# Routing attention and a gated feed-forward block on one core: score masks put ahead of their products, and two query tiles cut at 448 keys

## The chip, the cores and the metric

The kernel runs on one core of one Trainium2 chip. The metric is device time in microseconds (us) from the first to the last moment of one execution; the median of several runs is given. The engines are TensorE (PE; its weight loads are shown apart as PEld), VectorE (DVE), ScalarE (ACT), GpSimd (POOL) and SyncE (SP), which issues DMAs.

## The reference

Two blocks follow one another. The first is attention in which a query sees only the keys of its own cluster; the second is a feed-forward block with an activation of its own.

```
# B, H, S, D = 4, 8, 768, 64; 16 clusters for each head
q_assign = argmax(normalised q . normalised centroids)
k_assign = argmax(normalised k . normalised centroids)
mask   = q_assign[..., :, None] == k_assign[..., None, :]
scores = where(mask, q @ k.T / sqrt(D), -1e9)
scores = scores - max(scores, axis=-1)
attn   = exp(scores) / (sum(exp(scores)) + 1e-9)
x      = attn @ v, turned to (3072 tokens, 512)

h  = x @ w_in                       # 512 x 2048
sp = max(h, 0) + log1p(exp(-|h|))
out = (h * erf(sp)) @ w_out         # 2048 x 512
```

## The kernel before

The attention works on 16 pairs of heads (`p`), the two heads of a pair in the two halves of the 128 partitions (64 rows each). A pair has 6 tiles of 128 queries and 6 tiles of 128 keys. The program order of every engine is the order of the code (`InOrder`); nothing is reordered by a planner.

**Units.** A unit (`units`, line 542) is one half of the queries (384) against one tile of 128 keys; a pair has 12. Its scores lie in a tile `sc` of two PSUM banks, one for each head, and there are two such tiles (`ps_s`, line 177). `products(u)` multiplies keys by queries in float32 over 64 rows a head and opens the banks; `scores(u)` adds the cluster masks in bf16 and closes them; `curve(u)` takes the exponential on ACT and writes `pr`; `accumulate(u)` adds it up on POOL; `attend(u)` multiplies it with the values, one period later, into `turned`.

**The masks.** `km` holds the one-hot clusters of the keys and `qm` those of the queries, scaled so that their product is far below zero where clusters differ. They occupy 32 of the 64 rows of a head, and each of them is there twice: rows 0 to 31, where the first row of `qm` also holds the shift (the row maximum of the scores), and rows 32 to 63, without it. So `scores(u)` with 32 rows uses rows 0 to 31 of each half, and the maxima can use rows 32 to 63.

**The maxima.** Each query needs the maximum over its keys before its exponentials. `maxima_step` computes a piece: `passes("qv", "kv", ...)` multiplies a bf16 copy of 128 queries by some of the keys into the PSUM tile `wide` (two banks, one for each head; there is one such tile), `passes("qm", "km", ...)` adds the cluster masks, and DVE reduces the piece to a column of `nmx`. With `behind=True` it is a generator that stops between these parts, and its masks use rows 32 to 63; otherwise it runs through and they use all 64 rows. A query tile `t` is done in two pieces, the first over `KEYS[t]` keys and the second over the rest of the 768. After the second piece of tile 2 and tile 5, `into_rows` turns the maxima and four DMAs on SP's queue put them into `qm` as the shift of that half.

**A period.** `period(p, i)` (line 1393), six for each pair, runs two units, `u` and `u+1`, and two maxima steps. Its order on PE is

1. first step, run through (`step_ahead(p, 2*i)`): the second piece of a query tile, 64-row masks;
2. `products(u)`, `products(u+1)`;
3. second step (`step_ahead(p, 2*i+1, True)`): the first piece of the next query tile; its similarities, then `scores(u)`, then its masks, then `scores(u+1)`;
4. at some `i` a mask of the next pair (`masks`; at i=2 a narrow one in place 2, on 32 rows);
5. `attend` for the two units of the period before.

The steps of a period run ahead of the units that need them. For pairs from 1 on the pieces are, by period:

| i | first step: tile, keys before | second step: tile, keys before |
|---|---|---|
| 0 | 3, 256 | 4, 512 |
| 1 | 4, 256 | 5, 512 |
| 2 | 5, 256 | 0 of the next pair, 384 |
| 3 | 0, 384 | 1, 512 |
| 4 | 1, 256 | 2, 512 |
| 5 | 2, 256 | 3, 512 |

The feed-forward block after the attention is PE work in 128 by 128 tiles; the change does not touch it.

Of the kernel before, what the change touches and what calls it, by code (L numbers as in the profile page):

```python
# [9 lines left out]
F32 = mybir.dt.float32  # L10
# [9 lines left out]
P = 128  # L20
B, H, S, D = 4, 8, 768, 64
C = 16
NJ = S // P
Q = 32
NB = S // Q
HW = S // 2
QW = HW // 2
TW = QW + 1
HJ = NJ // 2
HP = H // 2  # L30
KEYS = (384, 512, 512, 512, 512, 512)
FIRST_KEYS = (256, 256, 352, 384, 256, 352)
JOINED = (
    ((0, 0, 0, 512),), ((0, 1, 512, 768), (1, 0, 0, 256)), ((1, 1, 256, 768),), ((2, 0, 0, 512),), ((2, 1, 512, 768),),
# [101 lines left out]
def kernel(  # L136
# [37 lines left out]
    def passing(name, bufs, **kw):  # L174
        return attention.enter_context(tc.tile_pool(name=name, bufs=bufs, **kw))

    ps_s = passing("ps_s", 2, space=PSUM)
# [30 lines left out]
    rows = [{nm: const.tile([P, S], F32, name=f"{nm}T{i}") for nm in "qk"} for i in range(2)]  # L208
# [109 lines left out]
    def sign(n):  # L318
        hi, _, upper = steps[n]
        ae.activation(out=upper, in_=hi, func=ACT.Prelu, scale=2.0**-25, alpha=2.0**90)  # L320
# [12 lines left out]
    for e in range(2):  # L333
        for n in range(2):
            r = e * D + n * Q
# [89 lines left out]
    def vectors(p, nm):  # L425
        if p < NPAIR:
            ae.copy(out=pairs[p][nm + "v"], in_=pairs[p][nm + "T"])

    def masks(p, nm, half, bank, narrow=False, copied_by=ae):

        if p >= NPAIR:
            return lambda: None
        st = pairs[p]
        cols = slice(half * HW, (half + 1) * HW)
        r, hot = slice(0, D) if nm == "q" else slice(D, P), st["hotT"]
        picked = pick[r, half]
        if narrow:
            r = slice(r.start + Q, r.stop)
            picked = pick[r, 1]
            hot = hot if half else st["aside"]  # L440
        won = bank[:, 0:HW]
        te.matmul(won, lhsT=picked, rhs=hot[r], start=True, stop=True)
        if nm == "q":
            return lambda: ae.activation(out=st["qm"][:, cols], in_=won, func=ACT.Relu)
        if copied_by is ve:
            return lambda: ve.tensor_scalar(
                out=st["km"][:, cols], in0=won, scalar1=BIG, scalar2=nbig, op0=ALU.mult, op1=ALU.add
            )
        return lambda: ae.activation(
            out=st["km"][:, cols], in_=won, func=ACT.Identity, bias=nbig, scale=BIG  # L450
        )
# [3 lines left out]
    def pieces_of(i, keys_of):  # L455
        t, part = divmod(i, 2)
        return ((t, part, *((0, keys_of[t]), (keys_of[t], S))[part]),)
# [84 lines left out]
    units = [(p, half, j) for p in range(NPAIR) for half in range(2) for j in range(NJ)]  # L542

    sc_of = {}

    def products(u):
        p, half, j = units[u]
        if u in sc_of:
            return
        st = pairs[p]  # L550
        sc = sc_of[u] = ps_s.tile([P, 2, 512], F32, name="sc", tag="s")
        for e in range(2):
            r = slice(e * D, (e + 1) * D)
            te.matmul(
                sc[:, e, 0:HW], lhsT=st["kT"][r, j * P : (j + 1) * P],
                rhs=st["qT"][r, half * HW : (half + 1) * HW], start=True, stop=False,
            )

    def scores(u, rows=Q):

        p, half, j = units[u]
        st = pairs[p]
        sc = sc_of[u]
        assert ("shift", half) in st
        for e in range(2):
            r = slice(e * D, (e + 1) * D)
            r = slice(r.start, r.start + rows)
            te.matmul(
                sc[:, e, 0:HW], lhsT=st["km"][r, j * P : (j + 1) * P],
                rhs=st["qm"][r, half * HW : (half + 1) * HW], start=False, stop=True,  # L570
            )

    def curve(u):
# [795 lines left out]
    def run(work):  # L1369
        for _ in work:  # L1370
            pass
# [3 lines left out]
    def step_ahead(p, i, behind=False):  # L1375
        if p == 0 and i < NJ:
            steps = maxima_step(0, pieces_of(NJ + i, FIRST_KEYS), behind=behind, by_products=True)
        elif p == 0 and i < NJ + len(JOINED):
            steps = maxima_step(1, JOINED[i - NJ], behind=behind)
        else:  # L1380
            p, i = divmod(2 * NJ * p + NJ + 1 + i, 2 * NJ)
            steps = maxima_step(p, pieces_of(i, KEYS), behind=behind) if p < NPAIR else iter(())
        if not behind:
            run(steps)
        return steps
# [7 lines left out]
    def period(p, i):  # L1393
        u = 2 * NJ * p + 2 * i
        n1, n2 = 2 * p - 1, 2 * p
        early = lambda n: 0 <= n < N_EARLY

        def mask(place):
            which = (MASKS if p else FIRST_MASKS).get((i, place))
            if which:  # L1400
                return masks(p + 1, *which, turned[0 if i in (0, 5) else 1], place == 2)
            return lambda: None

        if u > 0:
            for which in turns if i in (0, 3) else ():
                turn(*which)
                turns.remove(which)
            if i == 3 and not p:
                transposes(2, "k")
            if i == 3 and p:  # L1410
                similarities(p + 2)
                routing[0] = choose(p + 2, turned[0], True)
            step_ahead(p, 2 * i)
            if i == 3 and p:
                next(routing[0], None)
            if i == 2:
                transposes(p + 2, "k" if p else "q")
        mask(0)()
        if i == 0 and early(n1 - 1):
            sign(n1 - 1)  # L1420
        elif i == 3 and early(n1):
            sign(n1)
        if i == 4:
            next(routing[0], None)
        next(part[0], None)
        if i == 0 and p:
            run(routing[0])
            transposes(p + 2, "q")
        if u == 2:
            next(routing[0])  # L1430
        products(u)
        mask(3)()
        products(u + 1)
        mask(1)()
        second = step_ahead(p, 2 * i + 1, True) if u > 0 else iter(())
        next(second, None)
        rows = D if u == 0 or u + NJ + 2 >= len(units) else Q
        scores(u, rows)
        next(second, None)
        next(second, None)  # L1440
        next(part[0], None)
        if i == 5 or u == 2:
            next(routing[0], None)
        scores(u + 1, rows)
        later = mask(2)
        if i == 3 and not p:
            similarities(p + 2)
            routing[0] = choose(p + 2, turned[0], True)
        if i == 0:
            later()  # L1450
            curve(u)
        else:
            curve(u)
            later()
        curve(u + 1)
        if u == 0:
            step_ahead(0, 1)
            similarities(1)
            routing[0] = choose(1, turned[1])
            next(routing[0])  # L1460
            vectors(1, "q")
            vectors(1, "k")
        if i == 0 and early(n1 - 1):
            bounded(n1 - 1)
            shifted(n1 - 1)
        elif i == 1 and early(n1):
            size_and_rest(n1)
        elif i == 5 and early(n2):
            rest(n2)
        for _ in range(FORMS.get(p, {}).get(i, 0)):  # L1470
            x_forms.pop(0)() if x_forms else forms.pop(0)[0]()
        if i == 3:
            if not p:
                next(routing[0], None)
            if early(n1):
                bounded(n1)
                shifted(n1)
        elif i == 1:
            load(p + 1, "v", v, vp)
            if p == 0:  # L1480
                run(routing[0])
        elif i == 4:
            vectors(p + 2, "k")
            vectors(p + 2, "q")
        if u > 0:
            if i == 1 and early(n1 - 1):
                summed(n1 - 1)
            elif i == 4 and early(n1):
                summed(n1)
            if i in POOL_FORMS.get(p, ()) and forms:  # L1490
                forms.pop(0)[1]()
            for w in (u - 2, u - 1):
                accumulate(w)
            for w in (u - 2, u - 1):
                attend(w)
            if i == 3:
                next(routing[0], None)
            if i % HJ == 0 and u - 1 != LATE or u - 3 == LATE:
                part[0] = divide(u - 1 - u % NJ)
                next(part[0])  # L1500
        if i == 3 and early(n2):
            size(n2)
# [11 lines left out]
    st = pairs[0]  # L1514
# [56 lines left out]
    u = len(units)  # L1571
# [13 lines left out]
    behind = pool("behind", 1).tile([P, 1], F32, name="behind")  # L1585
# [87 lines left out]
```

## Time and profile before

| | |
|---|---|
| median of 3 runs | 947.51 us (947.37 to 947.69) |
| profiled execution | 948.0 us |
| its span, first to last instruction | 946.3 us |
| PE busy | 939.0 us, 99% |
| DVE busy | 785.0 us, 83% |
| ACT busy | 547.2 us, 58% |
| POOL busy | 505.6 us, 53% |

The time is that of the whole execution; the span is what the hardware profiler saw between the first and the last instruction of one execution. Every instruction that goes through the helper `InOrder` is recorded under its line, L127, so groups are told apart by their tiles: `wide<-kv,qv` are a maxima step's similarities, `wide<-km,qm` its masks, `sc<-qT,kT` the products (for every third pair the operands lie in `more_out`, and the row reads `sc<-more_out`), `sc<-qm,km` the score masks, `turned<-pr,in_v` the value products, `turned<-hotT,pick` a mask of the next pair in the making. A float32 matmul is recorded as two. The shape `64*128` says how many rows and columns of the array a matmul uses.

### The profile page before, as it was taken

Reading aid. Unit: us, or ns where it says so; the run is one execution under the profiler, and the core shown is the slowest. Engines: PE = TensorE matmul, PEld = TensorE weight load, DVE = VectorE, ACT = ScalarE, POOL = GpSimd, SP = SyncE. Lnnn points to the kernel's source line nnn. Section 1 sums busy time; section 2 is a strip of 40 time slices with the busy share of each in tenths; the row PEclk is TensorE's granted clock in tenths of the full one; section 3 lists DMA queues with packets and bytes.
Section 4 is the critical chain, followed back from the end, with each engine's and each line's share of the span. In section 5 each row is a group of like instructions: output and inputs, shape, how many; then the busy total and the mean of one; then the engine's idle time right before and its main releaser. Section 6 shows DMA issues by size and latency. Waiting matters only on the chain.

```text
span 946.3 us, 22340 instructions
## 1 busy us (share of the span) xinstructions
PE 939.0 (99%) x8764; PEld 708.1 (75%) x8764; DVE 785.0 (83%) x1420; ACT 547.2 (58%) x809; POOL 505.6 (53%) x357
## 2 busy tenths in 40 slices
PE   8999999999999999999999999999999999999998
PEld 3555555555555555588888888998999899989987
DVE  7888888888888887869886688689868977897887
ACT  3677777777777777476423543653257236525541
POOL 1688888888888888999118211450063016103600
PEclk9999999999999999999999999999999999999999
DMA  9354455445443621133876248353454336343533
GB/s 217 73 114 112 112 113 111 112 112 111 113 113 69 157 58 36 26 120 124 216 224 238 100 122 214 109 179 112 156 167 135 133 119 206 113 154 123 157 112 111
DMA packets 176352, 123.17 MB, mean 130 GB/s; under 512 B 132600, under 2 KB 143352, under 8 KB 176248
## 3 DMA queue, kind: packets, MB, share of 16 engines
q1 hardware_dynamic: 171880, 116.34, 43.1%
q0 software_dynamic: 1872, 4.98, 3.0%
q8 instruction: 69, 1.13, 0.5%
q10 hardware_dynamic: 2496, 0.43, 0.2%
q14 instruction: 35, 0.29, 0.1%
HBM read 91.78 MB, written 23.33 MB: 122 GB/s over the span
## 4 chain that ended last, share of the span: by engine, by line
PE 98%; DVE 1%; ACT 0%; issue 0%; DVEq 0%
PE bank L127 43%; PE turned L127 32%; PE sc L127 17%; PE wide L127 6%; DVE nmx L127 1%; ACT qm L127 0%; DVE sims L127 0%; ACT km L127 0%; DVE hotT L127 0%; DVE wide L127 0%; DVE hot L127 0%; DVE nbig L127 0%; DVE osb L127 0%; DVEq L1668 0%; DVE lowest L127 0%
## 5 line engine op out<-in xcount | busy, mean ns | idle before, releaser
L127 POOL TENSOR_TENSOR more_out<-more_out,pr 128x768 f32<-128x768 f32 x128 | 217.2, 1697 | 15.8 <-ACT pr L127 6.1
L127 DVE TENSOR_REDUCE nmx<-wide 128x2 f32<-128x512 f32 (+2 forms) x189 | 179.1, 948 | 46.9 <-PE wide L127 45.9
L127 ACT ACTIVATE pr<-sc 128x768 f32<-128x768 f32 x192 | 148.5, 810 | 80.5 <-PE wide L127 73.0
L127 PE MATMUL turned<-pr,in_v 128*32 128x193 f32 x3072 | 145.2, 330 | 0.0
L127 POOL TENSOR_TENSOR g<-g 128x512 f32<-128x512 f32 x36 | 47.2, 1310 | 180.7 <-DVE g L127 178.8
L127 PEld LDWEIGHTS turned<-pr,in_v 128*32 128x32 f32 x3072 | 90.2, 109 | 51.3 <-issue 27.3
L127 DVE TENSOR_TENSOR g<-g 128x512 f32<-128x512 f32 x132 | 90.8, 688 | 22.9 <-PE bank L127 12.2
L127 PE MATMUL sc<-qT,kT 64*128 64x384 f32 x528 | 98.5, 485 | 0.0
L127 DVE TENSOR_TENSOR g<-bank,g 128x256 f32<-128x256 f32 (+1 forms) x128 | 64.7, 531 | 18.1 <-PE bank L127 9.4
L127 PE MATMUL bank<-g_more,g 128*128 128x256 f32 (+1 forms) x328 | 75.8, 374 | 0.0
L127 PE MATMUL bank<-x_own,w_in 128*128 128x128 f32 (+1 forms) x440 | 74.0, 309 | 0.0
L127 ACT ACTIVATE a_s<-g 128x1024 f32<-128x1024 f32 x38 | 39.7, 1056 | 58.0 <-POOL g L127 45.3
L127 POOL TENSOR_TENSOR more_out<-pr,pr 128x768 f32<-128x768 f32 x32 | 59.6, 1864 | 20.1 <-ACT pr L127 20.1
L127 PEld LDWEIGHTS bank<-g_more,g 128*128 128x128 f32 x328 | 61.1, 190 | 8.4 <-DVE g L127 0.4
L127 DVE TENSOR_TENSOR g<-a_s,g 128x512 f32<-128x512 f32 x76 | 65.9, 888 | 0.9 <-ACT a_s L127 0.9
L127 PEld LDWEIGHTS bank<-x_own,w_in 128*128 128x128 f32 x440 | 63.2, 191 | 4.4 <-issue 0.6
L127 PE MATMUL wide<-kv,qv 64*128 64x256 bf16 (+2 forms) x378 | 64.8, 327 | 0.9 <-ACT km L127 0.6
L127 PE MATMUL bank<-w_out,g 128*128 128x256 f32 x280 | 64.5, 379 | 0.0
L127 PEld LDWEIGHTS <-qv 64*128 64x128 bf16 x384 | 23.1, 93 | 52.8 <-issue 37.8
L127 PE MATMUL wide<-km,qm 64*128 64x256 bf16 (+4 forms) x378 | 62.3, 326 | 0.0
L127 ACT ACT_TABLE_LOAD x40 | 51.3, 1283 | 17.6 <-DVE g L127 17.0
L127 PEld LDWEIGHTS sc<-qT,kT 64*128 64x128 f32 x528 | 46.3, 187 | 19.1 <-issue 1.8
(244 smaller groups left out, 1993.0 us busy)
## 6 DMA issues: line engine op xcount, KB each, us to landing
g_more<-b_dram SPq DMA_DIRECT2D x52, 512.0 KB
g_more<-w_dram SPq DMA_DIRECT2D x84, 256.0 KB
x_own<-in_moe_w_in_dram SPq DMA_DIRECT2D x13, 512.0 KB
in_v<-in_v_dram SPq DMA_DIRECT2D x32, 192.0 KB
x_dram<-more_out SPq DMA_DIRECT2D x128, 48.0 KB
x_own<-x_dram SPq DMA_DIRECT2D x6, 1024.0 KB
in_k<-in_k_dram SPq DMA_DIRECT2D x59, 96.0 KB
in_q<-in_q_dram SPq DMA_DIRECT2D x58, 96.0 KB
```

The lines of the kernel that those rows point to most:

```text
L127: ins = getattr(self.engine, name)(*args, **kw)
```

## The change

In four of the six periods (i = 1, 2, 4, 5) of pairs from 1 on, the score masks of the first unit go ahead of its products, between the similarities and the masks of the first maxima step. They open the banks (`start`), and the products, now behind them, close them (`stop`). The first step then runs as the second always did, with its masks on rows 32 to 63. In the second step only `scores(u+1)` is left beside the step's masks: it comes where `scores(u)` was, and the second call is left out. Periods 0 and 3 stay, since the shift of a new half comes in there, and so do pair 0 and the last periods of pair 15 (`more`).

Query tiles 2 and 5 are cut at 448 keys, so that their pieces are 448 and 320 keys, not 512 and 256. They are the second and the first step of periods 4 and 5, and of 1 and 2.

```diff
-KEYS = (384, 512, 512, 512, 512, 512)
+KEYS = (384, 512, 448, 512, 512, 448)
...
-    def products(u):
+    def score_banks(u):
+        if u not in sc_of:
+            sc_of[u] = ps_s.tile([P, 2, 512], F32, name="sc", tag="s")
+        return sc_of[u]
+
+    def products(u, behind=False):
         p, half, j = units[u]
-        if u in sc_of:
+        if u in sc_of and not behind:
             return
         st = pairs[p]
-        sc = sc_of[u] = ps_s.tile([P, 2, 512], F32, name="sc", tag="s")
+        sc = score_banks(u)
...
-                rhs=st["qT"][r, half * HW : (half + 1) * HW], start=True, stop=False,
+                rhs=st["qT"][r, half * HW : (half + 1) * HW], start=not behind, stop=behind,
...
-    def scores(u, rows=Q):
+    def scores(u, rows=Q, ahead=False):
...
-        sc = sc_of[u]
+        sc = score_banks(u)
...
-                rhs=st["qm"][r, half * HW : (half + 1) * HW], start=False, stop=True,
+                rhs=st["qm"][r, half * HW : (half + 1) * HW], start=ahead, stop=not ahead,
...
+        more = u + NJ + 2 < len(units)
+        ahead = p > 0 and i % HJ > 0 and more
...
-            step_ahead(p, 2 * i)
+            step = step_ahead(p, 2 * i, ahead)
+            next(step, None)
+            if ahead:
+                scores(u, Q, True)
+            run(step)
...
-        products(u)
+        products(u, ahead)
...
-        rows = D if u == 0 or u + NJ + 2 >= len(units) else Q
-        scores(u, rows)
+        rows = Q if u > 0 and more else D
+        scores(u + ahead, rows)
...
-        scores(u + 1, rows)
+        if not ahead:
+            scores(u + 1, rows)
```

## The prediction

> **What bounds the kernel now.** I read the page first: the span, the busy shares, the granted clock, the chain. Then a table of one long stretch, then the timeline of TensorE alone through single periods, then the other engines around the two places that the change touches.
>
> ```profile
> span 946.3 us, 22340 instructions
> PE 939.0 (99%) x8764; PEld 708.1 (75%) x8764; DVE 785.0 (83%) x1420; ACT 547.2 (58%) x809; POOL 505.6 (53%) x357
> PEclk9999999999999999999999999999999999999999
> PE 98%; DVE 1%; ACT 0%; issue 0%; DVEq 0%
> 39.00:387.00 348.00, 348.00 (x4953) 185.89 (x4947) 298.86 (x504) 267.77 (x402) 297.96 (x184) 1.00 0.44 99
> ```
>
> The last row is from the table of stretches: from 39 to 387 us, nearly all of the attention, PE is busy 348.00 of 348.00 us at a granted clock of 1.00; behind it stand PEld 185.89, DVE 298.86, ACT 267.77 and POOL 297.96. The chain of waits says the same: 98% PE. But "busy" includes modelled ends of matmuls, so what the array really loses must be read from when the next matmul starts. This is one period (i=5) on PE; columns are start, length, operation, and xN matmuls merged:
>
> ```profile
> 207.53 0.28 PE L127 MATMUL wide<-kv,qv 64*128 64x256 bf16 x2
> 207.65 0.27 PE L127 MATMUL wide<-km,qm 64*128 64x256 bf16 x2
> 207.75 1.46 PE L127 MATMUL sc<-qT,kT 64*128 64x384 f32 x8
> 209.05 0.38 PE L127 MATMUL wide<-kv,qv 64*128 64x512 bf16 x2
> 209.36 0.34 PE L127 MATMUL sc<-qm,km 32*128 32x384 bf16 x2
> 209.37 0.39 PE L127 MATMUL wide<-km,qm 32*128 32x512 bf16 x2
> 209.53 0.33 PE L127 MATMUL sc<-qm,km 32*128 32x384 bf16 x2
> 209.79 1.51 PE L127 MATMUL turned<-pr,in_v 128*32 128x193 f32 x32
> 211.23 0.28 PE L127 MATMUL wide<-kv,qv 64*128 64x256 bf16 x2
> ```
>
> Two rules come out of these starts. The shape 64*128 or 32*128 (rows x columns of the array) is the tiling. (a) Inside one tiling the next matmul follows after its predecessor's columns: 256 columns in about 0.11 (207.65 to 207.75), 384 in 0.17 (209.36 to 209.53), so 0.42 ns a column; matmuls on different row groups run side by side (209.36 and 209.37). (b) Where the tiling changes, the next row starts only 0.07 before the recorded end of the last one: 209.05+0.38 against 209.36, 209.53+0.33 against 209.79, 209.79+1.51 against 211.23. For 512 columns that is 0.31 where streaming takes 0.21, so a change of tiling costs 0.10. A period has three of them: 64 to 32, 32 to the 128*32 of the value products, and back.
>
> The Trainium skill says so as well: in TensorEngine Tiling, Key Properties, a change of tiling mode (not of tile alone) drains the array. It gives no time for it; the trace agrees, with the 0.10 above.
>
> **The first step of periods 1, 2, 4, 5.** Before, the clusters' masks of the first step use all 64 rows and stay in the tiling of the products that follow. In the changed kernel they use rows 32 to 63 of each half, with the scores' masks on rows 0 to 31: the tiling goes 64, 32, 64. So each such period gains two changes of tiling. The second change goes straight into the float32 products, and 32*128 to 64*128 float32 is nowhere in this trace. The nearest rows are near the end, where products follow value products:
>
> ```profile
> 388.58 0.67 PE L127 MATMUL turned<-pr,in_v 128*32 128x193 f32 x11
> 389.18 1.56 PE L127 MATMUL sc<-qT,kT 64*128 64x384 f32 x8
> 219.03 0.28 PE L127 MATMUL wide<-kv,qv 64*128 64x256 bf16 x2
> 219.26 0.81 PE L127 MATMUL sc<-more_out 64*128 64x384 f32 x4
> 220.97 0.34 PE L127 MATMUL sc<-qm,km 32*128 32x384 bf16 x2
> 220.97 0.33 PE L127 MATMUL wide<-km,qm 32*128 32x384 bf16 x2
> 221.14 0.32 PE L127 MATMUL sc<-qm,km 32*128 32x384 bf16 x2
> 221.15 0.32 PE L127 MATMUL turned<-hotT,pick 32*128 32x384 bf16 x1
> 221.40 1.35 PE L127 MATMUL turned<-pr,in_v 128*32 128x193 f32 x28
> ```
>
> The eight products take 1.56 there instead of 1.46: with no matmul of the same tiling before them, their first weights are loaded in the open, 0.10. I take 0.10; the lower bound is 0 (loaded ahead), and nothing suggests more.
>
> Step one before: 219.03 to 219.26, 0.23. Step one after, with 256 keys (i=1, 4): similarities 0.28-0.07 = 0.21; then the scores' masks, 384 columns, 0.34-0.07 = 0.27 (the step's own masks, 256 columns, run beside them); then the open load, 0.10. Together 0.58, so +0.35. With 320 keys (i=2, 5) the similarities stream 64 columns more, 0.03: +0.38.
>
> **The second step.** One of the two score masks has gone from it; what stays runs beside the step's masks. Before, from the similarities to the value products: 209.05 to 209.79, 0.74. After:
> - i=1, 4, 448 keys: similarities 0.38-0.03-0.07 = 0.28; masks 0.39-0.03, begun 0.01 late, less 0.07, 0.30. Sum 0.58, so -0.16.
> - i=5, 512 keys: 0.31, then 0.39+0.01-0.07 = 0.33, sum 0.64, so -0.10.
> - i=2, 384 keys: nothing. There a narrow mask of the next pair (221.15) stands behind. It needs the row group that the step's own masks hold, so 384+384 columns stay in a row there, just as the two score masks did before: 220.97 to 221.40 stays 0.43. Should the group be free, it is -0.16.
>
> **The sum.** Net: i=1 +0.19, i=2 +0.38, i=4 +0.19, i=5 +0.28; 1.04 a pair. Pairs 1 to 14 have all four, pair 15 only i=1 (after it no score masks go ahead): 14 x 1.04 + 0.19 = 14.8. In pair 15 at i=2 the old order meets 320 keys twice, +0.05. Total **+14.8 us**. The profiled execution took 948.0 us (span 946.3 and 1.7 around it), 0.5 over the median of 947.51; the sum put on the execution gives 962.8, on the median 962.3.
>
> **What else moves, and its cover.** DVE's maxima keep their sum: 512+256 keys become 448+320, two heads each.
>
> ```profile
> L127 DVE TENSOR_REDUCE nmx<-wide 128x2 f32<-128x1024 f32 x74 | 90.2, 1219 | 21.6 <-PE wide L127 21.6
> L127 DVE TENSOR_REDUCE nmx<-wide 128x2 f32<-128x512 f32 x74 | 50.9, 688 | 2.1 <-PE wide L127 1.1
> 207.69 0.55 DVE L127 SCALAR_TENSOR_TENSOR more_out<-den,turned 128x384 f32<-128x384 f32 x1
> 208.16 0.69 DVE L127 TENSOR_REDUCE nmx<-wide 128x2 f32<-128x512 f32 x1
> 209.44 2.21 SPq L127 DMA_DIRECT2D qm<-least_rows x4
> 213.66 0.58 ACT L127 ACTIVATE km<-turned,nbig 128x384 bf16<-128x384 f32 x1 [0.39 <-PE turned L127]
> 214.14 1.50 ACT L127 ACTIVATE pr<-sc 128x768 f32<-128x768 f32 x2
> 215.32 0.28 PE L127 MATMUL wide<-kv,qv 64*128 64x256 bf16 x2
> ```
>
> By the two group rows (mean 1219 and 688 ns) 128 elements are 0.13: the longer second piece takes 0.82, the shorter first one 1.09. The piece of i=5 is read from 208.16, once DVE has finished the row before it; PE's changed masks end about 0.54+0.02 after 207.53, at 208.1, so it starts about there and ends at 209.0. PE would overwrite the bank at 209.05+0.38 = 209.43. Cover 0.4, cost nothing. The shift rows that hang on this piece go out on SP (209.44, four DMAs) 0.13 later, but the score masks of i=0 that need them move back by 0.28: nothing.
>
> A score mask that goes ahead needs its bank freed by the exponential of two units earlier. The tightest place is i=1, since the mask copy at 213.66 comes first on ACT: the two exponentials run 214.14 to 215.64, so the first bank is free at 214.9. The mask would start at 215.32+0.21 = 215.53. The products that took that bank before started as early, so this adds no wait. Queued behind it on PE are the step's masks, the products and the value products, all of which would move with it. The first unit's exponential can start sooner, after its products; ACT has idle time there and nobody on the path waits for it, so it gains nothing.
>
> **Rivals.**
> *The loads are hidden.* The weights of the products are fetched during the masks, and only the two drains are paid: 57 x 0.10 = 5.7 less, +9.1, **956.6**. Against it: 1.56 at 389.18. For it: there the tiling came from another shape, 128*32. The Trainium skill has a rule that way, in TensorE: Matmul & The Clock Gate, The mechanism (Part 3): a weight load for a row group that does not conflict, or for the background buffer, is pulled ahead of matmuls in flight. The trace contradicts it wherever the tiling changes.
>
> *The change of tiling is free between 32 and 64 rows* (the other side, faster). Then only columns count, at 0.42 ns: i=1, 4 each 128 more in step one and 384 fewer in step two, -0.11; i=2 192 more, +0.08; i=5 192 more and 256 fewer, -0.03. A pair gains 0.17: 14 x 0.17 + 0.1 = 2.5, **945.0**. It decides if two changes and a load cost under 0.04 a period together, where I charge 0.30. Against it: 64 to 32 costs 0.10 at 209.36.
>
> *A new wait comes on top.* DVE's longer pieces in i=2 and i=5 reach PE after all (28 x 0.13 = 3.6), or the score mask at i=1 waits for both exponentials (15 x about 0.2 = 3): up to +18.4, **965.9**. Against it: the covers of 0.4 and 0.6 above.
>
> *The order does not change what runs together*: PE would hide it all, 947.5. Nothing in a stretch with PE busy 348.00 of 348.00 leaves room for that.
>
> **How the numbers follow.** Forecast as summed 0.80, loads hidden 0.08, a new wait 0.07, free tiling 0.03, no effect 0.02. A difference of 0.2%, 1.9 us, is what a measurement of this kernel can tell. So slower 0.95, same 0.02, faster 0.03. Inside the forecast, the free row group at i=2 would take 14 x 0.16 = 2.2 off, 960.1. The range runs from the hidden loads to the new wait: 956 to 966.
>
> **What would show it.** In the profile after: in i=1, 2, 4, 5 a row of 32*128 score masks between similarities and products, its start 0.21 (0.24) after the step's, the products 0.27 later and 1.56 long; from step one to the products 0.48 instead of 0.23; in step two 0.58 (i=1, 4) and 0.64 (i=5) instead of 0.74, and 0.43 kept after the masks' start at i=2. The attention ends about 15 us later, and everything after it is the same length. Wrong if the products start with no gap after masks of 32 rows, if PEld waits for ACT or DVE ahead of the score masks, or if the time beyond the attention changes.

## The result and the profile after

The changed kernel takes 961.97 us (median of 4 runs, 961.57 to 962.16) against 947.60 before: 14.37 us more, a ratio of 1.0151 (95% interval 1.0134 to 1.0169). The forecast was 962.3 and +14.8.

The page of the changed kernel, its span, its busy shares and its chain of waits by engine:

```profile
span 959.9 us, 22309 instructions
PE 952.3 (99%) x8764; PEld 713.5 (74%) x8764; DVE 783.1 (82%) x1420; ACT 552.1 (58%) x809; POOL 505.0 (53%) x357
PE 98%; DVE 1%; DMA 0%; SPq 0%; ACT 0%; issue 0%; DVEq 0%
```

PE is still the chain. Its busy time grew by 13.3 us with the same 8764 matmuls; DVE, ACT and POOL stay within 5 us of what they were. Where the time went is read from one stretch that begins and ends at the same instruction in both kernels: from the first step of pair 1, i=1, to the first step of pair 15, i=2. From the table of stretches, after and then before (start and end, length, then the busy time and count of PE, PEld, DVE, ACT and POOL):

```profile
47.31:399.53 352.22, 352.22 (x4807) 185.97 (x4804) 290.69 (x489) 264.96 (x391) 291.12 (x180) 1.00 0.43 98
```

```profile
47.92:385.79 337.87, 337.87 (x4807) 180.28 (x4804) 289.47 (x489) 259.77 (x391) 290.02 (x180) 1.00 0.45 102
```

The stretch is 352.22 us long in place of 337.87: 14.35 more, about all of the 14.37; behind it 560.4 us are left in the changed kernel and 560.5 in the one before. (The two profiled executions differ by 13.6 only: the one before, 948.0, lies 0.4 above its median, the changed one, 961.57, 0.4 below. In the changed one the stretch began 0.6 sooner, 47.31 against 47.92.) The timeline of PE in the changed kernel, i=1 and i=2 in a middle pair (two rows of i=2, the rest of the products and a mask beside them, are left out):

```profile
246.75 0.28 PE L127 MATMUL wide<-kv,qv 64*128 64x256 bf16 x2
246.96 0.34 PE L127 MATMUL sc<-qm,km 32*128 32x384 bf16 x2
246.97 0.28 PE L127 MATMUL wide<-km,qm 32*128 32x256 bf16 x2
247.23 1.56 PE L127 MATMUL sc<-qT,kT 64*128 64x384 f32 x8
248.62 0.36 PE L127 MATMUL wide<-kv,qv 64*128 64x448 bf16 x2
248.91 0.33 PE L127 MATMUL sc<-qm,km 32*128 32x384 bf16 x2
248.92 0.36 PE L127 MATMUL wide<-km,qm 32*128 32x448 bf16 x2
249.21 1.51 PE L127 MATMUL turned<-pr,in_v 128*32 128x193 f32 x32
250.66 0.31 PE L127 MATMUL wide<-kv,qv 64*128 64x320 bf16 x2
250.90 0.34 PE L127 MATMUL sc<-qm,km 32*128 32x384 bf16 x2
250.91 0.31 PE L127 MATMUL wide<-km,qm 32*128 32x320 bf16 x2
251.16 0.92 PE L127 MATMUL sc<-qT,kT 64*128 64x384 f32 x4
...
252.56 0.48 PE L127 MATMUL wide<-kv,qv 64*128 64x384 bf16 x2
252.97 0.33 PE L127 MATMUL sc<-qm,km 32*128 32x384 bf16 x2
252.98 0.34 PE L127 MATMUL wide<-km,qm 32*128 32x384 bf16 x2
253.16 0.32 PE L127 MATMUL turned<-hotT,pick 32*128 32x384 bf16 x1
253.41 1.51 PE L127 MATMUL turned<-pr,in_v 128*32 128x193 f32 x32
254.74 0.83 PE L127 MATMUL turned<-more_out,ccT 128*32 128x384 f32 x8
255.50 0.34 PE L127 MATMUL wide<-kv,qv 64*128 64x384 bf16 x2
```

Read the starts. Step one of i=1: similarities to score mask 0.21, masks to products 0.27, and the eight products last 1.56: the three terms of the forecast, as written. Step two: 248.62 to 249.21, 0.59 in place of 0.74 (forecast 0.58). At i=2 the narrow mask at 253.16 keeps the masks' stretch at 0.44 (252.97 to 253.41), where it was 0.43.

### The profile page after: what moved, and what is told of

Same layout as the page of the kernel before. It is cut to its first block, busy times and chain, and to the rows that moved or that the text cites. A ratio compares the mean times of both kernels' runs of the same rounds, so it can differ in the third digit from the quotient of the medians.

```text
span 959.9 us, 22309 instructions
## 1 busy us (share of the span) xinstructions
PE 952.3 (99%) x8764; PEld 713.5 (74%) x8764; DVE 783.1 (82%) x1420; ACT 552.1 (58%) x809; POOL 505.0 (53%) x357
## 4 chain that ended last, share of the span: by engine, by line
PE 98%; DVE 1%; DMA 0%; SPq 0%; ACT 0%; issue 0%; DVEq 0%
PE bank L127 42%; PE turned L127 32%; PE sc L127 19%; PE wide L127 5%; DVE nmx L127 1%; DMA in_k<-in_k_dram 0%; SPq L127 0%; DVE kT L127 0%; ACT qm L127 0%; DVE sims L127 0%; ACT km L127 0%; DVE hotT L127 0%; DVE wide L127 0%; DVE hot L127 0%; DVE osb L127 0%
## 5 line engine op out<-in xcount | busy, mean ns | idle before, releaser
L127 ACT ACTIVATE pr<-sc 128x768 f32<-128x768 f32 x192 | 153.0, 811 | 67.9 <-PE wide L127 42.4
L127 PE MATMUL sc<-qT,kT 64*128 64x384 f32 x528 | 102.4, 499 | 0.0
L127 PE MATMUL wide<-km,qm 32*128 32x256 bf16 (+5 forms) x378 | 62.7, 329 | 0.0
```

Source lines behind the costliest of these rows:

```text
L127: ins = getattr(self.engine, name)(*args, **kw)
```

## The experiments

All were compared with the kernel before, 947.58 us in each of the two sets. The edits are against the kernel named.

**Only the rows: the price of the changes of tiling alone.** Against before:

```diff
-            step_ahead(p, 2 * i)
+            run(step_ahead(p, 2 * i, p > 0 and i % HJ > 0 and u + NJ + 2 < len(units)))
```

> The order and the keys of before; only the masks of the first step in i=1, 2, 4, 5 use rows 32 to 63 of each half in place of all 64, as in after. Nothing is moved and no column is added or saved, so it prices two changes of tiling and the open load of the products by themselves. Theory: first step 0.21+0.21+0.10 in place of 0.23, +0.29, 57 times, 16.6 us, 964.2. Rival (loads hidden, drains paid): 57 x 0.19 = 10.9, 958.5. Rival (free tiling; the cost of after comes from the moved score masks): 947.6.

964.55 us, ratio 1.0177 (1.0162 to 1.0192): +16.97. Its timeline, i=1:

```profile
248.68 0.28 PE L127 MATMUL wide<-kv,qv 64*128 64x256 bf16 x2
248.90 0.28 PE L127 MATMUL wide<-km,qm 32*128 32x256 bf16 x2
249.11 1.56 PE L127 MATMUL sc<-qT,kT 64*128 64x384 f32 x8
```

The masks stream the same 256 columns, on 32 rows instead of 64. From step one to the products it is now 0.43 (248.68 to 249.11) instead of 0.23, and the products take 1.56 instead of 1.46: 0.30 a period with nothing moved. Neither free tiling (947.6 expected) nor hidden loads (958.5) survives this.

**Only the order**, with the keys of before:

```diff
-KEYS = (384, 512, 448, 512, 512, 448)
+KEYS = (384, 512, 512, 512, 512, 512)
```

(against after)

> The order of after with the tiles cut at 512 and 256 keys as before. Theory: step one +0.35 in all four periods, step two -0.10 in i=1, 4, 5 and 0 in i=2, where a wait of 0.03 for ACT also goes; 1.07 a pair, 15.2 us, 962.8, which is 0.8 above the whole change. Rival (DVE's longer pieces are part of the cost): 958.4, 3.6 below the whole change.

962.93 us, ratio 1.0161 (1.0146 to 1.0176): +15.35. So the order is the cost, and the keys take about 1 us off it. DVE's longer pieces cost nothing.

**Only the keys**, in the order of before:

```diff
-KEYS = (384, 512, 512, 512, 512, 512)
+KEYS = (384, 512, 448, 512, 512, 448)
```

> The order of before with the tiles cut at 448 and 320 keys. Theory (columns, changes of tiling, open weight loads): the second step saves 64 similarity columns in i=1 and i=4 (0.03 each; its masks stay hidden beside two score masks), the first step takes 128 columns more in i=2 and i=5 (0.05 each); 14 x 0.05 = 0.7 us, 948.3. Rival (the longer second pieces on DVE reach PE): 28 x 0.13 = 3.6 us, 951.2.

948.00 us, ratio 1.0004 (0.9995 to 1.0013): the interval holds no change and does not tell 0.7 from 0. It does exclude the rival's 951.2. The timeline shows the size, by the starts of the first steps of i=1, 2 and 3:

```profile
191.40 0.28 PE L127 MATMUL wide<-kv,qv 64*128 64x256 bf16 x2
...
195.08 0.31 PE L127 MATMUL wide<-kv,qv 64*128 64x320 bf16 x2
...
199.62 0.34 PE L127 MATMUL wide<-kv,qv 64*128 64x384 bf16 x2
```

i=1 takes 3.68 (it was 3.71 in before) and i=2 4.54 (4.50): a gain of 0.03 and a loss of 0.04 that nearly cancel, as do 0.03 and 0.05 in i=4 and i=5.

**One tiling: the score mask ahead, without a change of tiling.** Against after:

```diff
-        passes("qm", "km", False, slice(Q, D) if behind else slice(0, D))
+        passes("qm", "km", False, slice(Q, D) if behind and not full else slice(0, D))
...
-            step = step_ahead(p, 2 * i, ahead)
+            step = step_ahead(p, 2 * i, ahead, ahead)
...
-                scores(u, Q, True)
+                scores(u, D, True)
```

(`full` is handed through `step_ahead` to `maxima_step`.)

> After, but the score mask that goes ahead and the masks of the first step use all 64 rows of a head, so that the first step stays in the tiling of the products; score masks and step masks then stream one after the other. Theory: step one +384 columns (0.16) with 256 keys and +512 (0.21) with 320, no change of tiling, no open load; step two as in after. i=1 0, i=2 +0.18, i=4 0, i=5 +0.11; 14 x 0.29 = 4.1 us, 951.7. Rival (the price is in putting the score mask ahead: banks, order, waits): stays near after, 962, or above.

951.67 us, ratio 1.0042 (1.0025 to 1.0059): +4.09, to the tenth what the columns make. Its timeline, i=1:

```profile
192.97 0.28 PE L127 MATMUL wide<-kv,qv 64*128 64x256 bf16 x2
193.09 0.33 PE L127 MATMUL sc<-qm,km 64*128 64x384 bf16 x2
193.25 0.27 PE L127 MATMUL wide<-km,qm 64*128 64x256 bf16 x2
193.36 1.46 PE L127 MATMUL sc<-qT,kT 64*128 64x384 f32 x8
```

The masks now queue one behind the other, and still this is 0.19 shorter than in after: 0.39 from step one to the products (192.97 to 193.36) in place of 0.48, and products of 1.46 in place of 1.56. So putting the mask ahead of its products costs nothing by itself; the banks and the order of the two writes are not the price.

**Masks first: one change of tiling fewer, and the load covered.** Against after:

```diff
+        if turned_round:
+            passes("qm", "km", True, slice(Q, D))
+            passes("qv", "kv", False, slice(0, D))
+        else:
...
-            step = step_ahead(p, 2 * i, ahead)
-            next(step, None)
+            step = step_ahead(p, 2 * i, ahead, ahead)
             if ahead:
                 scores(u, Q, True)
```

(Behind `else` stand the lines of after; `turned_round` is handed through `step_ahead` to `maxima_step`.)

> After, but in the first step of i=1, 2, 4, 5 both masks on 32 rows (the score mask and the step's own) go ahead of the similarities, right behind the value products; the similarities close the banks and the products follow them in the same tiling. Same columns as after; one change of tiling fewer, and the products' first weights can be loaded during the similarities. Theory: step one 0.27+0.12 with 256 keys, 0.27+0.15 with 320, in place of 0.23: +0.16 and +0.19; step two as in after. i=1 0, i=2 +0.16, i=4 0, i=5 +0.09; 14 x 0.25 = 3.5 us, 951.1. Rival (the load stays open, only the drain goes): 57 x 0.10 more, 956.8. Rival (what costs is that the score mask goes ahead): as after, 962.

950.87 us, ratio 1.0035 (1.0022 to 1.0048): +3.29. Its timeline, i=1:

```profile
240.91 0.33 PE L127 MATMUL sc<-qm,km 32*128 32x384 bf16 x2
240.92 0.28 PE L127 MATMUL wide<-km,qm 32*128 32x256 bf16 x2
241.18 0.28 PE L127 MATMUL wide<-kv,qv 64*128 64x256 bf16 x2
241.30 1.46 PE L127 MATMUL sc<-qT,kT 64*128 64x384 f32 x8
...
243.17 1.51 PE L127 MATMUL turned<-pr,in_v 128*32 128x193 f32 x32
244.62 0.34 PE L127 MATMUL sc<-qm,km 32*128 32x384 bf16 x2
```

The same instructions in another order: the similarities now stand between the masks and the products, in the products' tiling. The products take 1.46 again, and a period of i=1 is 3.71 (240.91 to 244.62), the same as before. Where their weights are loaded stands in PEld's rows, of after and then of this run:

```profile
247.23 0.95 PEld L127 LDWEIGHTS sc<-qT,kT 64*128 64x128 f32 x8 [0.17 <-issue]
```

```profile
241.18 0.96 PEld L127 LDWEIGHTS sc<-qT,kT 64*128 64x128 f32 x8
```

In after the loads begin with the products (both at 247.23): the first is open. Here they begin with the similarities, 0.12 ahead of the products (241.18 against 241.30). Against after this run is 11.1 us faster, or 0.19 for each of the 57 periods: 0.10 of it is the open load (1.56 less 1.46), 0.09 the change of tiling (step one to the products, 0.48 less 0.39).

**Periods 1 and 4 alone.** Against after:

```diff
-        ahead = p > 0 and i % HJ > 0 and more
+        ahead = p > 0 and i % HJ == 1 and more
```

> After with the new order in i=1 and i=4 alone (keys as in after). Theory (each period pays for itself): +0.20 twice, and 0.05 in i=2 and i=5, where the old order meets 320 keys twice; 14 x 0.50 + 0.2 = 7.2 us, 954.8. Rival (periods share a cost, such as a wait that one period hands to the next): half of the change, 0.5 x 14.4, is about the same, so the timeline decides: i=1 3.91 and i=4 3.91 long, i=2 4.55 and i=5 3.76, or not.

954.57 us, ratio 1.0073 (1.0055 to 1.0091): +6.99. The starts of the first steps of i=1, 2, 3:

```profile
194.15 0.28 PE L127 MATMUL wide<-kv,qv 64*128 64x256 bf16 x2
...
198.06 0.31 PE L127 MATMUL wide<-kv,qv 64*128 64x320 bf16 x2
...
202.61 0.34 PE L127 MATMUL wide<-kv,qv 64*128 64x384 bf16 x2
```

i=1 is 3.91 long and i=2 4.55, and in the same timeline i=4 is 3.91 and i=5 3.76, all four as expected. The periods do not share a cost.

## Why the prediction was right

*TensorE bounds the attention, and what is put on it arrives whole.* Right, but for two small waits that went (below): 14.35 of 14.37 us lie in the stretch of the changed periods, and in all six experiments the time followed PE's columns and changes.

*Two more changes of tiling in a period, 0.10 each, and an open load of 0.10.* Right, and shown: "only the rows" prices them together (0.30 a period, +16.97), "one tiling" takes them away and leaves the columns (+4.09), "masks first" takes one change and the load (0.19 of 0.20). Two prices were taken from neighbouring rows. The change from 32 to 64 rows was not in the trace before and was charged like the other changes; "only the rows" shows it at the same 0.10. The open load was read behind value products; behind masks of 32 rows the products take the same 1.56.

*Loads and changes of tiling.* By the Trainium skill (TensorE: Matmul & The Clock Gate, The mechanism, Part 3) a weight load for a row group that does not conflict, or for the background buffer, is pulled ahead of matmuls in flight. Inside one tiling the trace agrees (loads 0.12 ahead, products of 1.46 behind the similarities); across a change of tiling, which that passage does not mention, nothing was pulled ahead (1.56). The Trainium skill's rule that a change of tiling mode drains the array (TensorEngine Tiling, Key Properties) gives no time; the trace agrees in so far as each change cost 0.10.

*The sum by periods.* Forecast +0.19, +0.38, +0.19, +0.28 for i=1, 2, 4, 5, and nothing for i=0 and 3. Measured i=1 3.91 (246.75 to 250.66) against 3.71: +0.20. i=2 4.84 (250.66 to 255.50); in before its similarities ran from 219.03 to those of i=3 at 223.53, 4.50: +0.34, 0.04 less than forecast. The means over pairs 1 to 13 are +0.20, +0.35, +0.20, +0.28, and i=3 is 0.03 shorter (4.19, in before 4.22). Two terms were off, and each is a wait of PE in before that went.

At i=2, PE waited for ACT ahead of the matmuls of a later pair with the centroids (between the value products and the first step of i=3), and their first weights were loaded in the open. The rows are of the kernel before, from PEld's timeline, PE's and ACT's; the bracket is the idle time and what ended it:

```profile
222.74 0.11 PEld L127 LDWEIGHTS turned<-qT,ccT 128*32 128x32 f32 x2 [0.20 <-ACT km L127]
223.53 0.34 PE L127 MATMUL wide<-kv,qv 64*128 64x384 bf16 x2
222.11 0.57 ACT L127 ACTIVATE km<-turned,nbig 128x384 bf16<-128x384 f32 x1
```

In after the mask copy (`km`) stands here:

```profile
253.52 0.58 ACT L127 ACTIVATE km<-turned,nbig 128x384 bf16<-128x384 f32 x1
```

It ends 0.06 ahead of these matmuls in before (222.68 against 222.74, where PE's row starts too) and 0.64 ahead in after (254.10 against 254.74). From the matmuls to the first step of i=3 it takes 0.76 in after (254.74 to 255.50), in before 0.79 (222.74 to 223.53). The forecast said the earlier exponential would gain nothing, as nobody on the path waits for it; but behind the exponential on ACT stands this copy, and at i=2 PE waits for that. The runs bear this out: the wait of 0.20 for `km` is in each of pairs 1 to 13 in before, "only the keys", "only the rows" and "periods 1 and 4 alone", and in none of after, "only the order", "one tiling" and "masks first", the four in which the score mask of i=2 goes ahead.

At i=3, PE waited in before for a sum of POOL's, in 9 of these 13 pairs:

```profile
203.35 0.16 PEld L127 LDWEIGHTS turned<-more_out,minus 128*32 128x32 f32 x8 [0.20 <-POOL more_out L127]
```

In after no pair has this wait. That the longer periods give POOL the time is likely but was not tried by itself.

The two make 0.06 a pair, some 0.8 us; the other periods came out about 0.03 a pair above the forecast, some 0.4. The difference is what the sum was too high by (14.8 against 14.4). So the mechanism was right, and that the total fits to 0.4 us is in part luck: the misses have opposite signs.

*DVE's cover.* The longer piece at i=5, on DVE in the changed kernel:

```profile
239.31 0.83 DVE L127 TENSOR_REDUCE nmx<-wide 128x2 f32<-128x640 f32 x1
```

It ends at 240.14. PE, in the same period, writes the bank anew at 240.57, and the cover is the 0.4 of the forecast:

```profile
238.67 0.31 PE L127 MATMUL wide<-kv,qv 64*128 64x320 bf16 x2
...
240.57 0.38 PE L127 MATMUL wide<-kv,qv 64*128 64x512 bf16 x2
```

*ACT's cover.* The exponentials that free the banks ahead of i=1, and the first one of i=1 itself:

```profile
245.56 1.50 ACT L127 ACTIVATE pr<-sc 128x768 f32<-128x768 f32 x2
...
248.25 0.81 ACT L127 ACTIVATE pr<-sc 128x768 f32<-128x768 f32 x1 [0.47 <-PE sc L127]
```

Half of 1.50 after 245.56 is 246.31; the score mask takes the bank at 246.96, so 0.65 to spare. The first exponential now follows the products: it waits for `sc`, the products' banks. In before the same one, at 217.59, waited for `wide`, masks that stand behind the products. That is as forecast.

*The rivals.* Free tiling and no effect are refuted by "only the rows"; a new wait by "only the keys" for DVE and by the rows above for ACT; hidden loads by the 1.56 in after and by PEld's rows, and the time they would have given, 956.6, was not reached.

No version faster than before came out of this. Of those with the new order "masks first" came nearest: it is level with before in i=1 and i=4, and its +3.29 lies mainly in i=2 and i=5 (4.65 and 3.79 in its timeline, against 4.50 and 3.70 before).

## What to carry to other kernels

Count changes of the array's tiling as instructions with a price of their own: here one cost 0.10, as much as streaming 240 columns at 0.42 ns each, so packing four matmuls side by side pays only if it saves more than that for every change it brings. Look at what comes first behind a change: with the float32 products there, 0.10 of their weight load was open, and a short bf16 matmul that was needed anyway hid it. Read such costs from start to start, since the busy share of PE was 99% before and after.

## What the runs showed of the hardware

Unexpected was only how even the price is. A change of tiling cost 0.10 us from 64 rows to 32 (in "only the rows" 248.68 to 248.90 is 0.22; inside one tiling it was 0.12) and, in "only the rows", from 32 to 64 (248.90 to 249.11 is 0.21 for 256 columns, which stream in 0.11). What stands first behind a change is also recorded longer: the products 1.56 against 1.46, which PEld's rows show to be their open load, and 256 columns of bf16 0.28 against 0.27, where the cause was not looked into.
